# A forward scan that starts from the heads' reciprocals, in a linear attention with two expert layers behind it

## The chip, the core and the metric

The kernel runs on one core of a Trainium2 chip. The metric is the device time of one execution in microseconds (us); lower is better. Each core has TensorE (PE in the profile, PEld for its weight loads), VectorE (DVE), ScalarE (ACT), GpSimd (POOL) and SyncE (SP, which only issues transfers here). Each engine runs its own program in order and waits on semaphores.

## The reference

Three layers, cut to what matters. The output of one is the input of the next.

```python
def _attn_ref(q, k, v, alpha):                 # 4 batches, 8 heads, 768 steps, 48 wide
    for t in range(S):
        state = alpha[:, :, t, :, None] * state + np.einsum('bhd,bhe->bhde', k[:, :, t], v[:, :, t])
        y[:, :, t] = np.einsum('bhd,bhde->bhe', q[:, :, t], state)

def _moe_ref(x, w_gate, w_noise, noise, w1, w2):   # 3072 tokens of 384, 8 experts, 1024 hidden
    noisy_logits = x @ w_gate + np.log1p(np.exp(x @ w_noise)) * noise
    top2 = np.argpartition(-noisy_logits, 2, axis=1)[:, :2]     # softmax over the two gives top2_w
    ...
            h = np.maximum(x[mask] @ w1[e], 0.0)
            out[mask] += top2_w[mask, k, None] * (h @ w2[e])

def _moe2_ref(x, w_in, w_out):                 # 384 -> 2048 -> 384
    h = x @ w_in
    return np.maximum(0.01 * h, h) @ w_out
```

## The kernel before

**Scan stage.** The 3072 steps are cut into 24 units of 128 steps (4 batches of 6). A unit holds all 8 heads: 48 channels of two heads on 112 partitions, four such pairs side by side, so a tile has 4 x 128 columns. With the decays `at`, VectorE makes two products by scans: backward `suf` (tile pF), the decay from a step to the unit's end, and forward `wt` (tile pT), the decay from the unit's start. Keys are multiplied by `suf` (kt), queries by `wt` (qp). A pattern in PSUM (pC, `ends` and `begins`) restarts the scans at each head. The forward scan starts from 1, and what is needed is `wt` divided by the head's total decay; VectorE takes the reciprocals of the four totals (rec), and ScalarE scales the queries with them, one ACTIVATE for each pair (`scaled`). TensorE then makes the scores (pS), GpSimd masks them (am), and further products give the unit's output (pY), its turned form (pA) and the state's update (pM).

**Route and passage.** For each four units the two best experts of each token are chosen by a chain of some 22 small VectorE operations (names g_, lg for the logits), TensorE counts (pA), and GpSimd scatters the rows to the experts' slots in DRAM (x_s, indexes si). After the sixth such group `gidx_op` computes `gidx`, the slots for the way back, and `top2_weights` the gate's weights; `fill_ops` (`free`, freesum, ...) finds the slots that stay empty.

**Experts.** Rows of an expert are loaded, transposed by TensorE (line 641, banks pA and pB in turn), and split into a high and a low part (xh by ScalarE, xl by VectorE) for three-product matmuls: `gemm1` (ph, nine matmuls a step), `gemm2` (py, three matmuls a block). The weights come in pairs of 256 hidden columns, four pairs an expert; ScalarE makes the high part (w1h, w2h), and VectorE or GpSimd the low part by a subtraction (`split_lo`, line 501; A and B are the buffers' names). Expert 0's low parts are made by GpSimd. Two groups of each expert and a dense third layer follow, all bound to the order below.

**Order.** Nothing is scheduled by hand: each piece of work is a step with an engine, a planned duration, needs and rings of buffers, and the `Planner` lays the steps out in time, engine by engine, and emits them in that order. Durations and due times decide only the order. A step with `port=True` on VectorE or GpSimd is not laid beside another such step of the other engine. `EARLY` is 2: experts 0 and 1 have a first group that is taken before all rows are known.

Of the kernel before, what the change touches and what calls it, by code (L numbers as in the profile page):

```python
# [7 lines left out]
FT = mybir.dt.float32  # L8
# [3 lines left out]
U32 = mybir.dt.uint32  # L12
# [68 lines left out]
class Planner:  # L81

    NEAR, FAR, SLACK, RATE, LAND = 0.1, 0.25, 0.8, 0.25, 2.0
# [282 lines left out]
def tile_kernel(  # L366
# [324 lines left out]
    def build_experts(t0, R, scat, last_x, ready_at, totals, acc_done, begun):  # L691
# [36 lines left out]
        def expert_weights(i, after):  # L728
# [4 lines left out]
            for m, nm in enumerate(("w1s", "w2s")):  # L733
# [5 lines left out]
                AUX[i].append([hi, add("vg" if phase == 2 else "g", dict(v=0.87, g=1.8) if phase == 2 else 1.8, lambda en="g", m=m: split_lo(i, m, en), [hi],  # L739
# [209 lines left out]
    with ExitStack() as actx:  # L949
# [4 lines left out]
        bank = psum.tile([PP, 2, HP, C // 4], U32, name="pC", bufs=1)  # L954
        nc.vector.memset(bank, 0)
        nc.vector.memset(bank[:, 0, :, C // 4 - 1:], 1 << 24)
        nc.vector.memset(bank[:, 1, :, 0:1], 1)
        ends, begins = (bank[:, i].rearrange("p h c -> p (h c)").bitcast(mybir.dt.uint8) for i in range(2))

        def keep_busy(area, n):  # L960
# [6 lines left out]
            scr=1, rec=4, pA=1, pB=1, xg=XGB, XT=2, W=NA + NB, w1s=2, w2s=2, ph=2, hh=4, hl=4, py=4, ys=3, hc=2, f64=F64B, f64o=2).items()}  # L967
# [6 lines left out]
        def build_unit(u):  # L974
# [29 lines left out]

            def back():
                d["suf"] = psum.tile([PP, NW], FT, name="pF", bufs=1)
                nc.vector.tensor_tensor_scan(rev(d["suf"][:, :]), rev(d["at"][:, 1:NW + 1]),
                                             rev(ends), 0.0, OP.mult, OP.add)
                d["sv"] = d["suf"].rearrange("p (h c) -> p h c", c=C)

            def forth():
                d["wt"] = psum.tile([PP, NW], FT, name="pT", bufs=1)
                nc.vector.tensor_tensor_scan(d["wt"][:, :], d["at"][:, 0:NW], begins, 0.0, OP.mult, OP.add)

            def inverse():
                d["rec"] = work.tile([PP, HP], FT, name="rec", bufs=4)
                nc.vector.reciprocal(d["rec"], d["sv"][:, :, 0])

            def total():
                nc.vector.tensor_mul(tots[:, u, :], d["sv"][:, :, 0], d["at"][:, NW + 1:NW + 1 + HP])  # L1020

            b0 = b1 = add("v", 1.13, back, use=[(LA, R["at"])], takes=[R["suf"]])
# [527 lines left out]
```

## Time and profile before

| | us |
|---|---|
| median of 3 runs | 1059.86 |
| lowest and highest run | 1059.13, 1061.74 |
| profiled execution, its own time | 1063.24 |
| its span, first to last instruction | 1061.50 |
| TensorE busy in the span | 1032.2 (97%) |
| VectorE, ScalarE, GpSimd busy | 572.0, 410.0, 256.5 |

The rows come from one profiled execution; times in them run from the start of its span. The scan stage lasts until about 150 us on TensorE, the experts follow without a break. Busy time of TensorE counts pipelined matmuls from start to modelled end. Idle time of an engine that is not the bound costs nothing by itself.

### The profile page before, as it was taken

To read this page: it belongs to the slowest core of one execution; us is meant where nothing else is said; L and a number is where in the kernel's file an instruction comes from. 1 tells how busy PE (TensorE), PEld (TensorE's weight loads), DVE (VectorE), ACT (ScalarE), POOL (GpSimd) and SP (SyncE) were. 2 spreads that over 40 slices of the span, in tenths; PEclk is the share of its full clock that TensorE was granted. 3 is DMA by queue.
4 is the path that set the end of the run, shared out by engine and by line. 5 is a ranking of instruction groups with operands and counts; after the bars stand their busy time and mean duration, and the time that the engine had idled before them with its cause. 6 is when DMAs were issued, how large, how long until landed. Compare 5 with 4: busy or idle time off the path is not lost.

```text
span 1061.5 us, 18105 instructions
## 1 busy us (share of the span) xinstructions
PE 1032.2 (97%) x6808; PEld 990.7 (93%) x6808; DVE 572.0 (54%) x1170; ACT 410.0 (39%) x911; POOL 256.5 (24%) x291
## 2 busy tenths in 40 slices
PE   8999997999999999999999999999999999999997
PEld 7877787989999999999899999999999999999997
DVE  6999946324455554656464224645454545454543
ACT  6988753324344535545453222322222222222211
POOL 3266676300122231325231021402020202000000
PEclk8999998999999999999999999999999999999999
DMA  9979445533553756657476352211010101000000
GB/s 240 236 229 293 144 141 178 173 118 127 162 189 118 223 159 191 199 174 230 140 240 212 103 198 97 82 38 38 31 45 23 45 23 46 23 16 23 1 24 25
DMA packets 77988, 132.59 MB, mean 125 GB/s; under 512 B 7890, under 2 KB 55380, under 8 KB 77892
## 3 DMA queue, kind: packets, MB, share of 16 engines
q1 hardware_dynamic: 71428, 111.49, 33.7%
q0 software_dynamic: 6464, 19.86, 5.7%
q8 instruction: 55, 0.90, 0.4%
q14 instruction: 41, 0.34, 0.1%
HBM read 93.18 MB, written 38.15 MB: 124 GB/s over the span
## 4 chain that ended last, share of the span: by engine, by line
PE 84%; DMA 5%; DVE 4%; ACT 3%; issue 2%; POOL 1%; SPq 0%; ACTq 0%; POOLq 0%; DVEq 0%
PE py L826 38%; PE ph L787 37%; PE pS L1069 2%; PE pY L1136 1%; DMA w_d<-f64g 1%; PE pA L641 1%; PE pA L1158 1%; PE pY L1129 1%; DMA w1s<-in_moe_w_dram 1%; PE pB L641 1%; DMA y_d<-ys 1%; DMA w2s<-in_moe_w_dram 1%; PE pM L1104 1%; DMA at<-in_al_l_dram 1%; DVE gidx L1276 1%
## 5 line engine op out<-in xcount | busy, mean ns | idle before, releaser
L797 ACT ACTIVATE hc<-ph 128x384 f32<-128x384 f32 x128 | 62.9, 491 | 292.3 <-PE ph L787 292.3
L811 DVE SCALAR_TENSOR_TENSOR hl<-ph,hh 128x384 fp32r<-128x384 f32 (+3 forms) x128 | 76.4, 598 | 182.3 <-ACT hh L804 182.1
L800 DVE SCALAR_TENSOR_TENSOR hc<-hc 128x384 f32<-128x384 f32 x128 | 71.5, 559 | 172.4 <-ACT hc L797 172.4
L804 ACT ACTIVATE hh<-ph 128x384 fp32r<-128x384 f32 (+3 forms) x128 | 66.8, 522 | 206.5 <-PE ph L787 199.1
L826 PE MATMUL py<-w2hA,hh 128*128 128x384 f32 (+2 forms) x416 | 142.6, 343 | 0.0
L826 PE MATMUL py<-w2hB,hh 128*128 128x384 f32 (+1 forms) x416 | 141.5, 340 | 0.3 <-ACT hh L804 0.3
L826 PE MATMUL py<-w2hA,hl 128*128 128x384 f32 (+2 forms) x416 | 141.1, 339 | 0.0
L826 PE MATMUL py<-w2lA,hh 128*128 128x384 f32 (+2 forms) x416 | 141.1, 339 | 0.0
L826 PE MATMUL py<-w2hB,hl 128*128 128x384 f32 (+1 forms) x416 | 140.0, 336 | 0.0
L826 PE MATMUL py<-w2lB,hh 128*128 128x384 f32 (+1 forms) x416 | 139.7, 336 | 0.0
L787 PE MATMUL ph<-xh,w1hB 128*128 128x384 f32 (+1 forms) x384 | 133.8, 348 | 2.6 <-DVE hl L811 2.6
L787 PE MATMUL ph<-xh,w1hA 128*128 128x384 f32 (+3 forms) x384 | 135.3, 352 | 0.7 <-DVE hl L811 0.7
L787 PE MATMUL ph<-xh,w1lA 128*128 128x384 f32 (+3 forms) x384 | 133.2, 347 | 1.8 <-POOL w1lA L501 1.8
L787 PE MATMUL ph<-xh,w1lB 128*128 128x384 f32 (+1 forms) x384 | 133.3, 347 | 0.0
L787 PE MATMUL ph<-xl,w1hB 128*128 128x384 f32 (+1 forms) x384 | 133.1, 347 | 0.0
L787 PE MATMUL ph<-xl,w1hA 128*128 128x384 f32 (+3 forms) x384 | 132.9, 346 | 0.0
L849 POOL DMA_INDIRECT xg<-y_d,gidx x48 | 49.3, 1027 | 315.7 <-PE pA L641 121.5
L814 DVE TENSOR_TENSOR hl<-hc,hh 128x384 fp32r<-128x384 f32 x128 | 71.5, 559 | 12.6 <-DVE hh L806 0.9
L826 PEld LDWEIGHTS py<-w2lA,hh 128*128 128x128 f32 (+2 forms) x416 | 77.2, 186 | 1.0
L826 PEld LDWEIGHTS py<-w2hB,hh 128*128 128x128 f32 (+1 forms) x416 | 77.1, 185 | 1.1 <-ACT hh L804 0.6
L826 PEld LDWEIGHTS py<-w2hA,hh 128*128 128x128 f32 (+2 forms) x416 | 77.2, 186 | 0.8
L826 PEld LDWEIGHTS py<-w2lB,hh 128*128 128x128 f32 (+1 forms) x416 | 77.0, 185 | 0.8
(166 smaller groups left out, 1847.7 us busy)
## 6 DMA issues: line engine op xcount, KB each, us to landing
w1s<-in_moe_w_dram SPq DMA_DIRECT2D x32, 384.0 KB
w2s<-in_moe_w_dram SPq DMA_DIRECT2D x32, 384.0 KB
kq<-in_kq_l_dram SPq DMA_DIRECT2D x24, 448.0 KB
nv<-in_v_l_dram SPq DMA_DIRECT2D x24, 256.0 KB
w1s<-in_moe_w_in_dram SPq DMA_DIRECT2D x24, 256.0 KB
w2s<-in_moe_w_out_dram SPq DMA_DIRECT2D x16, 384.0 KB
at<-in_al_l_dram SPq DMA_DIRECT2D x24, 226.2 KB
xg<-x_s SPq DMA_DIRECT2D x28, 174.0 KB
```

Of the source, the lines that this page charges most:

```text
L641: pe.last = nc.tensor.transpose(p[:, d, :n], src[:n, d * 128:(d + 1) * 128], identf[:n, :n])
L787: pe.last = nc.tensor.matmul(ps[:, :n], a[:, d, fo:fo + 128], x[:, d, :n], start=i == 0, stop=i == len(seq) - 1)
L797: nc.scalar.activation(hc[:, :n], ps[:, :n], AF.Copy)
L800: nc.vector.scalar_tensor_tensor(hc[:, :n], hc[:, :n], 0.01, hc[:, :n], op0=OP.mult, op1=OP.max)
L804: nc.scalar.activation(hh[:, :n], ps[:, :n], AF.Relu)
L811: nc.vector.scalar_tensor_tensor(hl[:, :n], ps[:, :n], 0.0, hh[:, :n].bitcast(FT), op0=OP.max, op1=OP.subtract)
L814: nc.vector.tensor_sub(hl[:, :n], HT[si, "hc"][:, :n], hh[:, :n].bitcast(FT))
L826: pe.last = nc.tensor.matmul(py[:n, :], h[:, o:o + n], w[:, f % 2, :], start=(f == 0 and i == 0), stop=(f == nf - 1 and i == 2))
L849: return nc.gpsimd.indirect_dma_start(out=yg, out_offset=None, in_=y_d[0:rows, :], in_offset=bass.IndirectOffsetOnAxis(ap=gidx[:, c, kk:kk ...
L1069: pe.last = nc.tensor.matmul(d["pa", i][:, p], d["kt"][r, p], d["qp"][r, p], start=True, stop=True)
L1104: pe.last = nc.tensor.matmul(d["pu"][r, p, :], d["kN"][:, p, r], d["v"][:, 2 * p + i, 0:D], start=p == 0, stop=first, skip_group_check=True)
L1129: pe.last = nc.tensor.matmul(d["py"][64 * i:64 * i + 64, p], d["v"][:, 2 * p + i, :], d["am"][:, i, p, :], start=p == 0, stop=first, skip_ ...
```

## The change

The pattern becomes a tile `heads` of zeros whose first column of each head is written anew for each unit: first 1.0 (`ones`, a memset of 4 elements for each partition) for the backward scan, then the reciprocal of the head's total (`inverse`, which now writes into `heads`) for the forward scan. So `forth` yields the scaled `wt` at once, `scaled` is gone, and `forth` needs `inverse`, which needs `back`. `suf` is one lasting tile. Besides, the planner reckons with a landing of 5 us instead of 2 for transfers of the second phase (rows, stores, reloads), the low parts of expert 1's weights are bound to VectorE, and `gidx_op` and `top2_weights` are marked `port=True`.

```diff
-    NEAR, FAR, SLACK, RATE, LAND = 0.1, 0.25, 0.8, 0.25, 2.0
+    NEAR, FAR, SLACK, RATE, LAND = 0.1, 0.25, 0.8, 0.25, (2.0, 5.0)
...
-                st.end = max(st.end, self.dma + self.LAND)
+                st.end = max(st.end, self.dma + self.LAND[st.phase - 1])
...
-                AUX[i].append([hi, add("vg" if phase == 2 else "g", dict(v=0.87, g=1.8) if phase == 2 else 1.8, lambda en="g", m=m: split_lo(i, m, en), [hi],
+                on = "g" if e == 0 else "v" if e < EARLY else "vg"
+                AUX[i].append([hi, add(on, dict(v=0.87, g=1.8) if len(on) > 1 else dict(v=0.87, g=1.8)[on],
+                                       lambda en=on[0], m=m: split_lo(i, m, en), [hi],
...
-        bank = psum.tile([PP, 2, HP, C // 4], U32, name="pC", bufs=1)
-        nc.vector.memset(bank, 0)
-        nc.vector.memset(bank[:, 0, :, C // 4 - 1:], 1 << 24)
-        nc.vector.memset(bank[:, 1, :, 0:1], 1)
-        ends, begins = (bank[:, i].rearrange("p h c -> p (h c)").bitcast(mybir.dt.uint8) for i in range(2))
+        heads = psum.tile([PP, HP, C], FT, name="pC", bufs=1)
+        suf = psum.tile([PP, HP, C], FT, name="pF", bufs=1)
+        nc.vector.memset(heads, 0.0)
+        nc.vector.memset(suf[:, HP - 1, C - 1:], 1.0)
+        heads_f, suf_f = (t.rearrange("p h c -> p (h c)") for t in (heads, suf))
...
+            def ones():
+                nc.vector.memset(heads[:, :, 0], 1.0)
+
             def back():
-                d["suf"] = psum.tile([PP, NW], FT, name="pF", bufs=1)
-                nc.vector.tensor_tensor_scan(rev(d["suf"][:, :]), rev(d["at"][:, 1:NW + 1]),
-                                             rev(ends), 0.0, OP.mult, OP.add)
-                d["sv"] = d["suf"].rearrange("p (h c) -> p h c", c=C)
+                nc.vector.tensor_tensor_scan(rev(suf_f[:, 0:NW - 1]), rev(d["at"][:, 1:NW]), rev(heads_f[:, 1:NW]),
+                                             1.0, OP.mult, OP.add)
+
+            def inverse():
+                nc.vector.reciprocal(heads[:, :, 0], suf[:, :, 0])
 
             def forth():
-                d["wt"] = psum.tile([PP, NW], FT, name="pT", bufs=1)
-                nc.vector.tensor_tensor_scan(d["wt"][:, :], d["at"][:, 0:NW], begins, 0.0, OP.mult, OP.add)
-
-            def inverse():
-                d["rec"] = work.tile([PP, HP], FT, name="rec", bufs=4)
-                nc.vector.reciprocal(d["rec"], d["sv"][:, :, 0])
+                d["wt"] = psum.tile([PP, HP, C], FT, name="pT", bufs=1)
+                nc.vector.tensor_tensor_scan(d["wt"].rearrange("p h c -> p (h c)"), d["at"][:, 0:NW], heads_f, 0.0,
+                                             OP.mult, OP.add)
...
-            f0 = f1 = add("v", 1.13, forth, use=[(LA, R["at"])], takes=[R["wt"]])
-            iv = add("v", 0.2, inverse, [b1], use=[(b0, R["suf"])], takes=[R["rec"]])
+            f0 = add("v", 1.13, forth, [iv], use=[(LA, R["at"]), (on, R["heads"])], takes=[R["wt"]])
...
-            def scaled():
-                for p in range(HP):
-                    nc.scalar.activation(d["qp"][:, p], d["qp"][:, p], AF.Copy, scale=d["rec"][:, p:p + 1])
...
-            q0 = add("v", 0.64, queries, [f1], use=[(LK, R["kq"]), (f0, R["wt"])], takes=[R["qp"]])
-            qq = add("a", 0.72, scaled, [q0], use=[(iv, R["rec"]), (q0, R["qp"])])
+            qq = add("v", 0.6, queries, use=[(LK, R["kq"]), (f0, R["wt"])], takes=[R["qp"]])
...
-            sc = add("p", 1.09, score, use=[(kk, R["kt"]), (q0, R["qp"])], deps=[qq], takes=[R["pS"], R["pT"]], due=b + 2.4, room=room_s)
+            sc = add("p", 1.09, score, use=[(kk, R["kt"]), (qq, R["qp"])], takes=[R["pS"], R["pT"]], due=b + 2.4, room=room_s)
...
             ends = [add("v", 0.15, gidx_op, [done_of["chain", gi][-1] for gi in range(len(RGROUPS))], phase=2,
-                        due=at_unit(NCH) + 150)]
+                        due=at_unit(NCH) + 150, port=True)]
             for eng, fn in top2_weights(nc, rt, lambda: m_all, wts[:, :, 0], wts[:, :, 1], NCH, "g_"):
-                ends.append(add(eng, 0.3, fn, ends[-1:], phase=2))
+                ends.append(add(eng, 0.3, fn, ends[-1:], phase=2, port=eng == "v"))
```

What the planner makes of it is shown at three places. First, one unit on VectorE near the start, before (forward scan pT, backward scan pF, queries qp, reciprocal rec, keys kt, total decay tots):

```order
L1013 SCALAR_TENSOR_TENSOR pT<-at,pC 112x512
L1007 SCALAR_TENSOR_TENSOR pF<-at,pC 112x512
L1034 TENSOR_TENSOR qp<-kq,pT 112x512
L1017 RECIPROCAL rec<-pF 112x4
L1030 TENSOR_TENSOR kt<-kq,pF 112x512
L1020 TENSOR_TENSOR tots<-pF,at 112x4
```

and after the change:

```order
L1008 MEMSET pC 112x4
L1011 SCALAR_TENSOR_TENSOR pF<-at,pC 112x511
L1015 RECIPROCAL pC<-pF 112x4
L1034 TENSOR_TENSOR kt<-kq,pF 112x512
L1019 SCALAR_TENSOR_TENSOR pT<-at,pC 112x512
L1023 TENSOR_TENSOR tots<-pF,at 112x4
L1038 TENSOR_TENSOR qp<-kq,pT 112x512
```

The backward scan goes first, a memset stands ahead of it, and the queries come last. Second, GpSimd in the passage, from the fourth scatter (x_s) behind the first weight splits on, before:

```order
L1257 DMA x_s<-xg,si 6785x384 x4
L501 TENSOR_TENSOR w1lA<-w1s,w1hA 128x768
L1257 DMA x_s<-xg,si 6785x384
L501 TENSOR_TENSOR w2lA<-w2s,w2hA 128x768
L1257 DMA x_s<-xg,si 6785x384
L501 TENSOR_TENSOR w1lA<-w1s,w1hA 128x768
L501 TENSOR_TENSOR w2lA<-w2s,w2hA 128x768
L501 TENSOR_TENSOR w1lB<-w1s,w1hB 128x768
L501 TENSOR_TENSOR w2lA<-w2s,w2hA 128x768
L1257 DMA x_s<-xg,si 6785x384 x8
```

and after:

```order
L1256 DMA x_s<-xg,si 6785x384 x4
L501 TENSOR_TENSOR w1lA<-w1s,w1hA 128x768
L1256 DMA x_s<-xg,si 6785x384
L501 TENSOR_TENSOR w2lA<-w2s,w2hA 128x768
L1256 DMA x_s<-xg,si 6785x384
L501 TENSOR_TENSOR w1lA<-w1s,w1hA 128x768
L501 TENSOR_TENSOR w2lA<-w2s,w2hA 128x768
L1256 DMA x_s<-xg,si 6785x384
L501 TENSOR_TENSOR w2lA<-w2s,w2hA 128x768
L1256 DMA x_s<-xg,si 6785x384 x7
```

The second w1lA of this piece is that of pair 3. The run behind it has lost w1lB, the first split of expert 1, and a scatter stands in its place. Third, TensorE at the count matmul (from acc and ones_b) whose result `free` reads, before:

```order
L578 MATMUL pA<-acc,ones_b 128x8
L826 MATMUL py<-w2hA,hh 112x384
L826 MATMUL py<-w2lA,hh 112x384
L826 MATMUL py<-w2hA,hl 112x384
L826 MATMUL py<-w2hA,hh 112x384
L826 MATMUL py<-w2lA,hh 112x384
L826 MATMUL py<-w2hA,hl 112x384
L641 MATMUL pA<-identf,xg 128x128 x3
```

After the change 18 such py rows and nine ph rows stand behind the count; the last of the nine and the transpositions are:

```order
L789 MATMUL ph<-xh,w1hA 128x336
L789 MATMUL ph<-xl,w1hA 128x336
L789 MATMUL ph<-xh,w1lA 128x336
L641 MATMUL pA<-identf,xg 128x128 x3
L641 MATMUL pB<-identf,xg 128x128 x3
```

The transposition into pA, which needs the bank that `free` reads, has moved 21 matmuls away from the count. On VectorE `gidx` and `free` still stand directly behind the last slots (si) and a subtraction for the expert.

## Rows read from the trace of the kernel before

**Rows 1.** Stretches: from:to, length, busy by engine (instructions), TensorE clock, DMA share, GB/s.

```profile
0.00:138.00 138.00, 128.38 (x1637) 109.32 (x1638) 119.89 (x282) 108.19 (x293) 69.94 (x116) 0.96 0.78 224
138.00:180.00 42.00, 34.27 (x265) 31.95 (x265) 20.84 (x56) 14.69 (x32) 30.46 (x25) 0.92 0.47 156
180.00:1054.00 874.00, 868.12 (x4903) 848.38 (x4902) 431.28 (x833) 285.63 (x585) 156.14 (x151) 1.00 0.34 108
```

**Rows 2.** Waits of TensorE up to 200 us: total, times, longest.

```profile
PE pA L641 <- DVE free L582: 4.9, 1, 4.9
PE ph L787 <- POOL w1lA L501: 1.8, 1, 1.8
```

**Rows 3.** Chain that ended last, behind 170 us: start, length, what.

```profile
171.26 2.88 PE py L826 x9
...
174.14 2.29 PE ph L787 x9
176.43 1.59 PE py L826 x9
```

**Rows 4.** Stretches of TensorE alone: length, busy, granted clock, DMA share, GB/s.

```profile
12.40:19.00 6.60, 6.60 (x56) 0.50 1.03 253
...
175.00:176.00 1.00, 1.00 (x5) 0.50 0.50 115
```

**Rows 5.** VectorE in order of time: start, length, line, operation, tiles.

```profile
164.05 6.08 DVE L1276 SCALAR_TENSOR_TENSOR gidx<-pk_all,cm_all 128x48 uint32<-128x48 f32 x1
...
170.15 0.15 DVE L582 TENSOR_SCALAR free<-pA 128x8 f32<-128x8 f32 x1
```

**Rows 6.** GpSimd in order of time, the same stretch.

```profile
163.71 0.99 POOL L1257 DMA_INDIRECT x_s<-xg,si  x1 [0.17 <-issue]
...
168.25 1.81 POOL L501 TENSOR_TENSOR w1lB<-w1s,w1hB 128x768 fp32r<-128x768 f32 x1
```

**Rows 7.** Groups up to 160 us: busy, mean ns | idle before, releasers.

```profile
L1038 ACT ACTIVATE qp<-qp,rec 112x128 f32<-112x128 f32 x96 | 30.6, 394 | 7.9 <-DVE rec L1017 6.6 <-DVE qp L1034 0.9 <-DVE g_z L264 0.3
```

**Rows 8.** Groups of VectorE up to 138 us, as above.

```profile
L1017 DVE RECIPROCAL rec<-pF 112x4 f32<-112x4 f32 x24 | 4.1, 172 | 0.1
...
L284 DVE TENSOR_REDUCE cm_all<-g_ca 128x4 f32<-128x32 f32 x10 | 1.9, 186 | 0.3
...
L956 DVE MEMSET pC<- 112x4 uint32 x1 | 0.1, 62 | 0.1
```

**Rows 9.** VectorE in order of time, an early unit and the last.

```profile
22.48 1.20 DVE L1007 TENSOR_TENSOR_SCAN pF<-at,pC 112x512 f32<-112x512 f32 x1
23.78 0.18 DVE L1017 RECIPROCAL rec<-pF 112x4 f32<-112x4 f32 x1
23.88 0.13 DVE L1020 TENSOR_TENSOR tots<-pF,at 112x4 f32<-112x4 f32 x1
...
134.39 0.68 DVE L1030 TENSOR_TENSOR kt<-kq,pF 112x512 f32<-112x512 f32 x1
```

**Rows 10.** Waits of VectorE up to 138 us.

```profile
DVE lg L1167 <- ACT xg L1162: 5.4, 8, 1.7
DVE pT L1013 <- DMA at<-in_al_l_dram: 5.1, 2, 2.9
...
DVE lg L1167 <- PE pA L1158: 1.1, 2, 0.6
```

**Rows 11.** TensorE in order of time, the end of the scan stage.

```profile
138.00 1.16 PE L1069 MATMUL pS<-qp,kt 48*128 48x128 f32 x16
...
140.17 1.09 PE L1129 MATMUL pY<-am,nv 128*64 128x128 f32 x16
...
149.52 0.40 PE L787 MATMUL ph<-xh,w1hA 128*128 128x336 f32 x1
...
153.78 0.34 PE L826 MATMUL py<-w2hA,hh 128*112 128x384 f32 x1
```

**Rows 12.** TensorE in order of time, the rows of expert 2.

```profile
212.19 0.52 PE L641 MATMUL pA<-identf,xg 116*128 116x116 f32 x3 [0.72 <-DVE xl L650]
```

More of the change, by code (lines that the diff above doesn't have):

```diff
@@ L966, in tile_kernel @@
             at=5, kq=4, nv=5, suf=1, wt=1, kt=4, qp=4, pM=1, kN=2, pS=1, pT=1, ar=2, am=2, sp=2, S=2, pY=1, xt=XTB,
-            scr=1, rec=4, pA=1, pB=1, xg=XGB, XT=2, W=NA + NB, w1s=2, w2s=2, ph=2, hh=4, hl=4, py=4, ys=3, hc=2, f64=F64B, f64o=2).items()}
+            scr=1, heads=1, pA=1, pB=1, xg=XGB, XT=2, W=NA + NB, w1s=2, w2s=2, ph=2, hh=4, hl=4, py=4, ys=3, hc=2, f64=F64B, f64o=2).items()}
         add = plan.add
@@ L1022, in build_unit @@
-            b0 = b1 = add("v", 1.13, back, use=[(LA, R["at"])], takes=[R["suf"]])
-            tt = add("v", 0.12, total, [b1], use=[(LA, R["at"]), (b0, R["suf"])])
+                d["wt"] = psum.tile([PP, HP, C], FT, name="pT", bufs=1)
+                nc.vector.tensor_tensor_scan(d["wt"].rearrange("p h c -> p (h c)"), d["at"][:, 0:NW], heads_f, 0.0,
+                                             OP.mult, OP.add)
+            def total():
+                nc.vector.tensor_mul(tots[:, u, :], suf[:, :, 0], d["at"][:, NW + 1:NW + 1 + HP])
@@ L1024, in build_unit @@
+            on = add("v", 0.07, ones, takes=[R["heads"]])
+            b0 = add("v", 1.13, back, use=[(LA, R["at"]), (on, R["heads"])], takes=[R["suf"]])
+            iv = add("v", 0.1, inverse, use=[(b0, R["suf"]), (on, R["heads"])])
+            tt = add("v", 0.09, total, use=[(LA, R["at"]), (b0, R["suf"])])
             totals.append(tt)
-            f0 = f1 = add("v", 1.13, forth, use=[(LA, R["at"])], takes=[R["wt"]])
-            iv = add("v", 0.2, inverse, [b1], use=[(b0, R["suf"])], takes=[R["rec"]])
+            f0 = add("v", 1.13, forth, [iv], use=[(LA, R["at"]), (on, R["heads"])], takes=[R["wt"]])
@@ L1040, in build_unit @@
-            kk = add("v", 0.64, keys, [b1], use=[(LK, R["kq"]), (b0, R["suf"])], takes=[R["kt"]])
-            q0 = add("v", 0.64, queries, [f1], use=[(LK, R["kq"]), (f0, R["wt"])], takes=[R["qp"]])
-            qq = add("a", 0.72, scaled, [q0], use=[(iv, R["rec"]), (q0, R["qp"])])
+                nc.vector.tensor_mul(d["qp"], d["kq"][:, 1], d["wt"])
+            kk = add("v", 0.59, keys, use=[(LK, R["kq"]), (b0, R["suf"])], takes=[R["kt"]])
+            qq = add("v", 0.6, queries, use=[(LK, R["kq"]), (f0, R["wt"])], takes=[R["qp"]])
@@ L1095, in decay @@
                     nc.gpsimd.tensor_mul(d["sp"], prev["S"], tots[:, u, :, None].to_broadcast([PP, HP, D]))
-                dc = add("g", 0.42, decay, [tt], use=[(prev["step"], R["S"])], takes=[R["sp"]], port=True)
+                dc = add("g", 0.47, decay, [tt], use=[(prev["step"], R["S"])], takes=[R["sp"]], port=True)
             if not last:
@@ L1142, in build_unit @@
             if not first:
-                done = add("p", 1.01, across, [w0, qq], use=[(q0, R["qp"]), (dc, R["sp"]), (w0, R["pY"])],
+                done = add("p", 1.01, across, [w0], use=[(qq, R["qp"]), (dc, R["sp"]), (w0, R["pY"])],
                            due=b + PERIOD + 5)
```

4 lines of the change are left out of this document (1 added, 3 removed).

## The prediction

> **What bounds the kernel now.** I read the stretches first, to see where TensorE is not busy. From 180 us to the last product it misses 5.9 of 874; before 138 it misses 9.6 us, and between 138 and 180 it misses 7.7 with a mean granted clock of 0.92 [rows 1]. So the experts' part is TensorE's own work, and what lies behind 1054 us is the last store, and the change can only win in the first 180 us, the scan stage and the passage from it to the experts. In the scan stage VectorE is nearly as full as TensorE: 119.89 of 138 us [rows 1].
>
> Next the waits of TensorE up to 200 us. The longest is one of 4.9 us: a transposition of expert rows into the bank pA waited for VectorE's `free`. The second, 1.8 us, waited for a weight split (w1lA) on GpSimd [rows 2]. Before the long wait TensorE ran at its full clock of 2.4 GHz; behind it the granted clock was 0.50 of that, 1.2 GHz, up to 176 us, and nine products that take 1.59 us at the full clock took 2.88 us [rows 3, 4].
>
> Then I looked at what `free` waited for. It stands on VectorE behind `gidx`, a tiny operation that lasted from 164.05 to 170.13 [rows 5]. In those 6.08 us GpSimd ran a scatter and then three weight splits with nothing between them, of 1.8 us each; the last ended at 170.06 [rows 6]. `gidx` came through exactly when GpSimd's run of splits was over, so the 4.9 us are a collision of VectorE and GpSimd, and the halved clock is its consequence.
>
> **The passage, the sure part.** Three edits meet here. `gidx` and the operations on the gate's weights are marked as users of the shared port, so the planner lays no GpSimd step beside them; expert 1's splits may run on VectorE alone, which takes the split w1lB out of GpSimd's run (VectorE, busy 20.84 of 42 us there [rows 1], has room for it); and the new order moves TensorE's steps. The listings show the result: `gidx` still stands behind the last slots of the route, but GpSimd's run behind the scatter is two splits and then a scatter, and TensorE has 18 products (py) and 9 (ph) between the count and the transposition that needs `free`, where it had 6 py.
> If `gidx` meets the run again at the same point, it ends with the second split, 1.8 us after the end of the split of pair 3 (w1lA). TensorE's last 9 ph ahead of the transposition need that same split, and they take some 1.4 us (27 of them stood between 149.52 and 153.78 together with nothing else, 0.158 us each [rows 11]). So what is left of the 4.92 us is about 0.4, wherever the run lies; if `gidx` is free of the run, nothing. I take 4.5 us.
> The clock gives back more. The products at 171.26 lost 2.88 less 1.59, 1.3 us; those at 174.14 took 2.29 where nine at 0.158 take 1.42, 0.9 us; the transposition ahead some 0.3 [rows 3]. That is 2.5 us, and **the passage gives 7.0 us**, at most 7.4.
> The Trainium skill says in "SBUF — State Buffer", section "Who interferes with whom", that an instruction with two SBUF inputs on VectorE and a GpSimd instruction that reads SBUF exclude each other, the second blocking until the first is done. By that rule `gidx` would have waited for one split, 1.8 us at most, while the trace shows three. By the rule nothing would be left of the wait now, and the passage would give 7.4 instead of 7.0.
> The 1.8 us behind w1lA [rows 2] I leave as they are: GpSimd's order is unchanged up to that split (two splits, one, four scatters, this one), and the whole row hangs on the same slots of the route as TensorE's way there.
>
> **The scan stage, the unsure part.** Removed are 24 times four ScalarE operations, 30.6 us of ScalarE [rows 7]. They lie between the forward scan and the scores, but ScalarE is not the bound: it is busy 108.19 of 138 us [rows 1]. Added to VectorE is one memset of 4 elements for each unit; the scans, the reciprocal and the two products stay. What is new is the order of need: memset, backward scan, reciprocal, forward scan, queries, each needing the one before. Before, the two scans had no need of each other.
> The trace has this price. Behind a backward scan of 1.20 us that ended at 23.68, the reciprocal that needs it began at 23.78, 0.10 after its end; the next operation, which does not need the reciprocal, began 0.07 before the reciprocal's end [rows 9]. A need costs 0.17 us. For each unit: a memset, 0.06 [rows 8], with the backward scan 0.10 behind it, together 0.16; the reciprocal right behind its scan, 0.17; the queries behind the forward scan, 0.17 less the 0.08 of a small product that mostly stands between, 0.09. The sum is 0.42, and 24 units make 10.1 us. From below it is the memsets alone, 24 by 0.06 or 1.5 us; from above, three full needs and the memset for each unit, 24 by 0.57 or 13.7 us.
> The Trainium skill says in "VectorE: DVE Perf Modes", section "The DRAIN you can't avoid", that a semaphore between chained operations costs nothing extra, since the pipe is emptied anyhow. The rows just read differ. By the rule only the 1.5 us of memsets are added, and that case is a rival below.
> What takes this up is VectorE's own idle time. It waited 5.4 us for ScalarE's copies ahead of the logits (lg), 1.1 us in the same place for TensorE, and 5.1 us for the first loads of decays, of which some 2.2 lie ahead of the first scan [rows 10]. A slower VectorE meets the loads and copies later, and ScalarE, 30.6 us lighter, copies sooner: 9.4 us could be recovered, I take 8. So VectorE comes 2.1 us later to its end.
> The last unit counts. Before, its keys were ready at 135.07 [rows 9], behind 14 small operations of the fifth route and one subtraction for the expert; in the new listing its last operand, the queries, has 9 of them and no subtraction ahead. Five at 0.22 (0.19 and the gap [rows 8]) and 0.5 make 1.6 us. So the operand is ready at 135.07 + 2.1 - 1.6 = 135.6, and the last score can start at 135.7 instead of 138.00 [rows 11], 2.3 earlier. Of that about 0.9 is lost again: the route's count matmul is four steps further on TensorE, and VectorE has 11 small operations and two subtractions of 0.5 to do for it behind the queries, 3.6 us, while TensorE needs 1.16 + 0.6 + 1.1 to get there. **The scan stage ends 1.4 us earlier**; in general its end moves by the added time less the recovered less 3.5.
>
> **Edits that I cost at nothing.** The later landing (5 us instead of 2 for transfers of the second phase) changes TensorE's order behind the passage at three places: one pair of steps swapped, the transpositions ahead of the dense layer later by a step or two, and those of expert 2 closer together. The first two are hidden by TensorE's queue, which has 5.9 us of gaps in 874 [rows 1]. For the third there is a price: the transpositions into two banks already waited 0.72 us for VectorE's subtraction [rows 12], and one product of 0.5 us fewer stands between them. I add 0.5 us. The load of values is one place earlier on SP, which could shorten the first gap; taken as nothing.
>
> **Sum.** 7.0 + 1.4 - 0.5 = 7.9 us. The profiled execution took 1063.24 us for a span of 1061.50, the median of the runs is 1059.86; so 1055.3 in such an execution and **1052.0 us** in the median. A change under 0.3%, 3.2 us, can't be told from none.
>
> **The rivals.**
> *VectorE becomes the bound of the scan stage.* Its logits' waits stay, because the copies wait for TensorE and not for ScalarE, and only 4 us are recovered. The stage ends 10.1 - 4 - 3.5 = 2.6 us later; 7.0 - 2.6 - 0.5 = 3.9 us, 1056.0. For it speaks that VectorE is 87% busy [rows 1]; against it that most of those waits name ScalarE. Chance 0.20.
> *The collision is only moved.* `gidx` is not let in at the scatter between the second and the third split: it ends 1.8 + 1.0 + 1.8 = 4.6 us after the split that TensorE's 9 ph need, TensorE waits 3.2 us, and the clock falls again. The passage gives 1.7 us, in all 2.6, 1057.3. For it speaks that `gidx` was already held during the scatter ahead of the splits [rows 5, 6]. Chance 0.10.
> *Slower.* The small operations on VectorE's new chain are held up as others are: the memset and reciprocal write into PSUM while scans read it, and each unit pays 1.0 us instead of 0.42. Then 24 - 8 - 3.5 = 12.5 us are lost in the scan stage, and 1065.9 comes out; it turns slower than 3.2 us from 0.88 us a unit on. Against it: 24 reciprocals have a mean of 172 ns, with no long one to pull it up [rows 8]. Chance 0.07.
> *Needs cost nothing.* Only the memsets are added. 1.5 - 8 - 3.5 would be 10 us earlier, but TensorE can't follow: it has 9.6 us of idle time in 138 [rows 1], a part of it ahead of its first work. I take 4 us of it: 7.0 + 4 - 0.5 = 10.5, 1049.4. The reciprocal at 23.78 speaks against it [rows 9]. Chance 0.06. The section on the DRAIN in the Trainium skill's page "VectorE: DVE Perf Modes" would have it so.
> *The early clock stays up.* Behind the gaps of the start, TensorE worked without a pause from 12.4 to 19.0 us at a granted clock of 0.50, 1.2 GHz [rows 4]; half of the 6.6 us is lost. If the earlier start of unit 1 avoids that, 3.3 us come on top: 1048.7. Chance 0.07.
>
> **How the numbers follow.** My forecast has a chance of 0.50 and its own range of 1048.5 to 1056, from 6 to 9.4 us recovered and 8 to 12 added. The range of 1046.5 to 1058.5 takes in all but the slow rival and the outer parts of the second and last. Faster than 1056.7: nearly all of the forecast, the two fast rivals, half of the first and a little of the second, 0.75. Slower than 1063.0: the slow rival, 0.06. The rest, 0.19, is no change.
>
> **What the profile after will show.** The passage: `gidx` at 4 us or less, no wait of TensorE for `free` above 0.5 us, and the clock at 1.00 from 160 to 180. The scan stage: reciprocals some 0.10 behind the end of the backward scan; VectorE busier than 87% of the stage, with less waiting at lg; ScalarE near 78 us busy; the first ph between 146 and 149.5. From 220 us on the two traces should run in step. I am wrong if the first ph comes later than 150, or if `free` is still what a transposition waits for.

## The result and the profile after

The changed kernel takes 1048.53 us in the median, against 1060.8 for the kernel before beside it: a ratio of 0.9886, interval 0.9861 to 0.9912. A second set gave 0.9909 (0.9883 to 0.9934). So it is some 10 to 12 us faster; forecast were 7.9, with 1052.0 us and a range of 1046.5 to 1058.5. The profiled execution took 1047.05 us (span 1045.3), 16.2 less than the one of before (1063.24), which lay high among its kind (four timed runs of it gave 1059.13 to 1062.08).

Stretches of the changed kernel, columns as in [rows 1], the last up to its last product:

```profile
0.00:138.00 138.00, 126.83 (x1678) 107.22 (x1678) 125.43 (x307) 85.76 (x200) 72.27 (x119) 0.99 0.83 227
138.00:180.00 42.00, 39.54 (x280) 37.05 (x276) 26.96 (x64) 19.46 (x38) 33.36 (x29) 1.00 0.63 207
180.00:1038.00 858.00, 855.59 (x4847) 837.33 (x4846) 421.01 (x821) 278.37 (x573) 157.90 (x149) 1.00 0.33 107
```

From 0 to 138 us ScalarE has lost 22 us of work, VectorE is busy for 125.4 us instead of 119.9, and the granted clock is 0.99 instead of 0.96. From 138 to 180 TensorE is busy for 39.5 instead of 34.3 us at a full clock. Behind 180 us it misses 2.4 of 858 us; before it was 5.9 of 874. Waits of TensorE up to 200 us:

```profile
PE pA L1230 <- DVE lg L1166: 3.9, 3, 1.5
...
PE ph L789 <- DVE acc L1219: 1.2, 1, 1.2
```

The two rows of [rows 2] are gone, `free` and w1lA. Where the one for w1lA was, 1.2 us ahead of a ph are left; the waits ahead of the route's rank product (L1230) for `lg`, all in the scan stage, have grown from 1.5 us to 3.9. The passage on VectorE, then on GpSimd, then on TensorE:

```profile
159.85 4.38 DVE L1275 SCALAR_TENSOR_TENSOR gidx<-pk_all,cm_all 128x48 uint32<-128x48 f32 x1
164.16 0.15 DVE L582 TENSOR_SCALAR free<-pA 128x8 f32<-128x8 f32 x1
```

```profile
160.50 1.86 POOL L501 TENSOR_TENSOR w1lA<-w1s,w1hA 128x768 fp32r<-128x768 f32 x1
162.30 1.85 POOL L501 TENSOR_TENSOR w2lA<-w2s,w2hA 128x768 fp32r<-128x768 f32 x1
164.32 0.99 POOL L1256 DMA_INDIRECT x_s<-xg,si  x1 [0.17 <-issue]
```

```profile
160.30 0.17 PE L578 MATMUL pA<-acc,ones_b 128*128 128x8 bf16 x1
...
164.94 0.49 PE L641 MATMUL pA<-identf,xg 128*128 128x128 f32 x3
```

`gidx` still meets the run, but the run ends with its second split at 164.15, and `gidx` at 164.23; the scatter behind it begins at 164.32. `free` is done at 164.31, and the transposition into pA, 27 matmuls behind the count, begins at 164.94 without a wait. This is the passage as forecast (rows 5, 6 and 3 of before answer to it).

To see where the time came from I read one and the same matmul in both traces: the first ph, the 163rd and the last.

| profiled execution | first ph | first to 163rd | 163rd to last |
|---|---|---|---|
| before | 149.52 | 67.40 | 833.36 |
| changed | 146.61 | 60.81 | 826.66 |
| difference | 2.9 | 6.6 | 6.7 |
| forecast | 1.4 | 6.5 | 0 |

The 0.5 us that I took off for expert 2 belongs to the middle stretch, since its transpositions come before the 163rd ph (212.19 and 216.92 us before).

The last stretch is a surprise. Waits of TensorE behind 200 us, before and then changed:

```profile
PE ph L787 <- DVE hl L811: 3.3, 3, 1.8
PE pB L641 <- DVE xl L650: 1.3, 1, 1.3
PE pA L641 <- DVE xl L650: 0.7, 1, 0.7
```

```profile
PE pA L641 <- DVE xl L650: 1.6, 2, 0.9
PE pA L641 <- PE pB L641: 0.8, 1, 0.8
```

Before, these and two of 0.3 us made 5.9. The 0.7 and one of the 0.3 belong to expert 2's transpositions, ahead of the 163rd ph, as do 1.6 of the changed kernel's 2.4. So 4.8 us stand against 0.9 behind it. Besides, before had a granted clock of 0.50 from 531.0 to 534.4 us, which cost some 1.7 us; the changed kernel has no such place there. About 1 us of the 6.7 is left that I can't place.

The largest step, 3.5 us, lies near 530 us. VectorE, then TensorE, before:

```profile
529.55 0.56 DVE L834 COPY ys<-py 116x384 f32<-116x384 f32 x1 [3.48 <-issue]
530.02 0.55 DVE L811 SCALAR_TENSOR_TENSOR hl<-ph,hh 128x384 fp32r<-128x384 f32 x1
```

```profile
530.62 0.44 PE L787 MATMUL ph<-xh,w1hB 128*128 128x384 f32 x1 [1.76 <-DVE hl L811]
```

The subtraction `hl` stood on VectorE behind a copy of results (ys), ahead of which VectorE was idle for 3.48 us, and its operand `hh` was ready at 528.34 at the latest. The halved clock follows that wait. The place of the 1.3 us shows the same of `xl`, before:

```profile
293.60 0.96 DVE L501 TENSOR_TENSOR w2lB<-w2s,w2hB 128x768 fp32r<-128x768 f32 x1 [2.34 <-ACT w2hB L497]
294.47 0.51 DVE L650 TENSOR_TENSOR xl<-pB,xh 128x348 fp32r<-128x348 f32 x1
```

```profile
295.04 0.52 PE L641 MATMUL pB<-identf,xg 116*128 116x116 f32 x3 [1.30 <-DVE xl L650]
```

and changed:

```profile
281.31 0.52 DVE L650 TENSOR_TENSOR xl<-pB,xh 128x348 fp32r<-128x348 f32 x1
284.43 0.96 DVE L501 TENSOR_TENSOR w2lB<-w2s,w2hB 128x768 fp32r<-128x768 f32 x1 [2.60 <-ACT w2hB L497]
```

```profile
284.10 0.46 PE L641 MATMUL pB<-identf,xg 116*128 116x116 f32 x3
```

Before, the subtraction `xl` stood on VectorE behind one for w2lB, whose weights had just landed; now `xl` comes first, at 281.31, and TensorE's transposition at 284.10 waits for nothing. This order is the planner's, and the edit that moves it is the landing of 5 us, whose moves behind the passage I had costed at nothing.

### The profile page after: what moved, and what is told of

It reads as the page before. It is cut to its first block, busy times and chain, and to the rows that moved or that the text cites. A ratio compares the mean times of both kernels' runs of the same rounds, so it can differ in the third digit from the quotient of the medians.

```text
span 1045.3 us, 18038 instructions
## 1 busy us (share of the span) xinstructions
PE 1023.1 (98%) x6800; PEld 982.5 (94%) x6800; DVE 573.4 (55%) x1190; ACT 385.1 (37%) x814; POOL 263.5 (25%) x295
## 4 chain that ended last, share of the span: by engine, by line
PE 87%; DMA 5%; DVE 5%; ACT 1%; issue 1%; SPq 0%; DVEq 0%; ACTq 0%
PE py L828 40%; PE ph L789 39%; DMA at<-in_al_l_dram 2%; PE pY L1128 1%; DMA kq<-in_kq_l_dram 1%; PE pA L641 1%; PE pA L1157 1%; PE pY L1135 1%; PE pB L641 1%; PE pS L1068 1%; DMA w2s<-in_moe_w_dram 1%; DMA nv<-in_v_l_dram 1%; DVE pF L1011 0%; PE pM L1107 0%; PE pM L1103 0%
## 5 line engine op out<-in xcount | busy, mean ns | idle before, releaser
L799 ACT ACTIVATE hc<-ph 128x384 f32<-128x384 f32 x128 | 62.9, 491 | 289.6 <-PE ph L789 287.0
```

The lines of the kernel that those rows point to most:

```text
L799: nc.scalar.activation(hc[:, :n], ps[:, :n], AF.Copy)
```

## The experiments

Three sets, each with its own runs of the kernel before beside it (medians 1061.5, 1060.15 and 1056.48 us, on three chips). A gain over the kernel before is worked out from the ratio; two kernels of one set are compared by their medians. My theory after the result: the landing gives all behind 220 us, in the passage the landing (a later transposition) and the split binding (a shorter run) each take part of one wait, and the scan's restart itself may be worth nothing. Rivals: the late waits were chance; the restart gives the 2.9 us.

**Landing alone.**

```diff
-    NEAR, FAR, SLACK, RATE, LAND = 0.1, 0.25, 0.8, 0.25, 2.0
+    NEAR, FAR, SLACK, RATE, LAND = 0.1, 0.25, 0.8, 0.25, (2.0, 5.0)
...
-                st.end = max(st.end, self.dma + self.LAND)
+                st.end = max(st.end, self.dma + self.LAND[st.phase - 1])
```

> The kernel before with one edit, the landing of 5 us in the planner's second phase. Theory (order): the transposition into pA that needs `free` now stands 15 py and 9 ph behind the count instead of 6 py, 3.0 us further, and GpSimd's run still holds three splits, so its wait falls from 4.9 us to about 2; behind 220 us VectorE and ScalarE take the rows of an expert ahead of weights that have not landed, and the later waits for xl and hl (0.7 to 1.8 us each) and the halved clock near 531 us are gone, 6 us. In all 8 to 11.5 us faster than before, 1049 to 1053. Rival (chance of the loads): the later waits belong to one execution and not to the order; then only the passage gains, 3 to 5.5 us, and waits for xl or hl of 4 us in all stand in the profile behind 220 us. Rival (nothing): the planner's numbers move no wait; within 1 us of before.

Measured: 1051.33 us, 0.9902 (0.988 to 0.9923), 10.4 us faster. One constant gives most of the whole change. VectorE and GpSimd in its passage:

```profile
161.13 6.17 DVE L1247 SCALAR_TENSOR_TENSOR si<-pk_all,cm_all 128x8 uint32<-128x8 f32 x1 [0.18 <-issue]
...
167.64 0.19 DVE L1276 SCALAR_TENSOR_TENSOR gidx<-pk_all,cm_all 128x48 uint32<-128x48 f32 x1
```

```profile
165.46 1.81 POOL L501 TENSOR_TENSOR w1lB<-w1s,w1hB 128x768 fp32r<-128x768 f32 x1
```

Here it was `si`, ahead of `gidx`, that met the run; it ended at 167.30, when the third split did (167.27). The wait for `free` was 2.2 us, as expected, and no wait above 0.3 us was left behind 220 us.

**Split binding and marks alone.**

```diff
+                on = "g" if e == 0 else "v" if e < EARLY else "vg"
...
-                        due=at_unit(NCH) + 150)]
+                        due=at_unit(NCH) + 150, port=True)]
```

> The kernel before with the two passage edits alone: expert 1's low parts on VectorE, and the port marks. The transposition stays 6 py behind the count. Theory: `gidx` ends with the second split of GpSimd's run instead of the third, 1.8 us earlier; the wait for `free` falls from 4.9 to about 3.1 us and the clock falls to 0.50 behind it all the same; 1.5 to 2.5 us faster. Rival (my prediction's credit for these two edits and the order together): `gidx` is let in at once by the marks, the wait is under 0.5 us, 7 us faster. Rival (only moved): `gidx` is held over the scatter and one more split, the wait stays at 4.9 us or grows, no change.

Measured: 1056.68 us, 0.9946 (0.9926 to 0.9965), 5.7 us faster, more than the theory's 1.5 to 2.5 and less than the rival's 7.

```profile
164.94 3.94 DVE L1278 SCALAR_TENSOR_TENSOR gidx<-pk_all,cm_all 128x48 uint32<-128x48 f32 x1
```

```profile
167.00 1.81 POOL L501 TENSOR_TENSOR w2lA<-w2s,w2hA 128x768 fp32r<-128x768 f32 x1
```

```profile
PE pA L641 <- DVE free L582: 1.5, 1, 1.5
```

`gidx` took 3.94 us and ended at 168.88 with the second split (168.81), as the theory has it; but the wait was 1.5 us, not 3.1, and the clock, at 0.50 from 162 to 165 us, was 0.99 in the ten behind that. Besides, 18 products and not 6 stood between expert 2's transpositions, and their 1.0 us of waits was gone. The rule of the run holds; what the wait costs also hangs on where TensorE is when the run begins, which I had not priced.

**Restart alone**, with the two other edits taken back.

```diff
+            def ones():
+                nc.vector.memset(heads[:, :, 0], 1.0)
...
-            qq = add("a", 0.72, scaled, [q0], use=[(iv, R["rec"]), (q0, R["qp"])])
+            qq = add("v", 0.6, queries, use=[(LK, R["kq"]), (f0, R["wt"])], takes=[R["qp"]])
```

> The kernel before with the restart from the reciprocals alone (memset, new order of need, no scaling on ScalarE). Theory: the scan stage behaves as in the changed kernel, the first ph comes 2.9 us earlier than in the kernel before, with the granted clock at 1.00 from 12 to 19 us; the wait for `free` stays, 4.9 less about 0.5 us for three more py ahead, and the clock falls to 0.50 behind it; the waits behind 220 us stay. 2.5 to 4 us faster. Rival (the early clock is chance): the clock falls at 12 us here too, and the stage ends as before or up to 0.5 us later; within 1 us of before. Rival (the restart carries the gain): 7 us or more faster.

Measured: 1058.65 us, 0.9978 (0.9961 to 0.9994), 2.3 us faster: small, but more than nothing. The first ph came at 148.30, and the clock fell at 16.7 us all the same, so neither the theory nor its first rival fits; the wait for `free` was 3.9 us, where 4.4 were expected. Its middle stretch is 66.21 us, 1.2 shorter than before.

**The changed kernel without the landing.**

```diff
-    NEAR, FAR, SLACK, RATE, LAND = 0.1, 0.25, 0.8, 0.25, (2.0, 5.0)
+    NEAR, FAR, SLACK, RATE, LAND = 0.1, 0.25, 0.8, 0.25, 2.0
```

> The changed kernel with the landing of 2 us everywhere. Theory (three separate gains): the first ph 2.9 us earlier; the transposition stands 9 py behind the count, `gidx` ends with the second split, so about 2.5 us of wait and the halved clock stay; the waits behind 220 us stay. 5 to 6.5 us faster than before, so 6 us slower than the changed kernel. Rival (landing does nothing): as the changed kernel, 12 us faster. Rival (the split and the marks give all of the passage): 9.5 to 10.5 us faster.

Measured: 1055.99 us, 0.9936 (0.9913 to 0.9958), 6.8 us faster than before (5.5 by the medians). Its late stretch is 831.06 us, 4.4 longer than the changed kernel's. Its first ph, at 150.88, is the latest of the first six traces though its scans are the new ones, with the clock at 0.50 from 15.8 to 22.6 us: the restart does not keep the early clock up.

**The changed kernel without the restart** (the old scans and `scaled`, all else changed; no diff beyond the one shown).

> The kernel before with the landing, the split binding and the port marks, but the old scans and ScalarE's scaling: the changed kernel without its headline. Theory (the restart is worth nothing in the end of the scan stage; the 2.9 us in the profiled pair were an early halved clock that falls or doesn't fall by execution): landing alone gave 10.4 us and left 2.2 us of wait for `free`, which the shorter run of splits takes away, so 12 to 13 us faster than before, level with the changed kernel within 1 us. Rival (my prediction's term, 1.4 us from the stage): 1 to 2 us slower than the changed kernel. Rival (2.9 us from the stage, as the pair of traces has it): 3 us slower than the changed kernel or more.

Measured: 1050.13 us, 0.9899 (0.9878 to 0.992), beside 0.9909 for the changed kernel in the same set; the theory had 12 to 13 us over the kernel before, and it is 10.7. Level: without the restart the kernel is 0.2 us faster by the medians, inside the intervals, and beside the other edits no gain of the restart shows. VectorE does wait less with it. Its longest waits up to 138 us in this kernel, and then in the changed kernel's second trace:

```profile
DVE lg L1169 <- ACT xg L1164: 7.0, 8, 3.8
DVE pT L1015 <- DMA at<-in_al_l_dram: 3.6, 2, 2.4
```

```profile
DVE lg L1166 <- ACT xg L1161: 3.3, 4, 1.8
DVE pF L1011 <- DMA at<-in_al_l_dram: 2.4, 1, 2.4
```

**The changed kernel without the split binding.**

```diff
-                on = "g" if e == 0 else "v" if e < EARLY else "vg"
...
+                AUX[i].append([hi, add("vg" if phase == 2 else "g", dict(v=0.87, g=1.8) if phase == 2 else 1.8, lambda en="g", m=m: split_lo(i, m, en), [hi],
```

> The changed kernel with expert 1's low parts on either engine as before, so the run of GpSimd behind the scatter is three splits again; the transposition stays 18 py and 9 ph behind the count. Theory (the lock is held for the whole run): `gidx` or the `si` ahead of it ends with the third split, 1.8 us later than in the changed kernel, where the transposition began 0.6 us behind `free`; so a wait of about 1.2 us, and 1 to 3 us slower than the changed kernel, by whether the clock falls. Rival (one split blocks): no wait, level with the changed kernel. Rival (the split binding carries the passage): 5 us slower or more.

Measured: 1052.77 us, 0.9925 (0.9901 to 0.9949), 2.4 us slower than the changed kernel beside it. That is the size that the theory of the run has, but the two intervals overlap, so the time alone does not show it. The trace does, VectorE, GpSimd and TensorE:

```profile
162.41 7.93 DVE L1273 SCALAR_TENSOR_TENSOR gidx<-pk_all,cm_all 128x48 uint32<-128x48 f32 x1
```

```profile
168.47 1.79 POOL L501 TENSOR_TENSOR w2lA<-w2s,w2hA 128x768 fp32r<-128x768 f32 x1
```

```profile
170.47 0.55 PE L641 MATMUL pA<-identf,xg 128*128 128x128 f32 x3 [2.81 <-DVE free L582]
```

With the run now four splits, `gidx` lasted 7.93 us and ended at 170.34; the fourth split ended at 170.26.

**Six memsets a unit.**

```diff
-                nc.vector.memset(heads[:, :, 0], 1.0)
+                for _ in range(6):
+                    nc.vector.memset(heads[:, :, 0], 1.0)
```

> The changed kernel with six memsets of the heads' columns a unit instead of one, in the same order on every engine. Each more costs VectorE between 0.06 us (its duration) and 0.16 us (with a gap behind it), so 24 x 5 x 0.06 to 0.16 = 7 to 19 us in all. Theory (VectorE bounds the scan stage, with some 5 us of its idle time still to be had up to 138 us): 2 to 14 us slower than the changed kernel, and the first ph later by as much. Rival (TensorE bounds it, VectorE has room): within 1 us of the changed kernel.

Measured: 1068.91 us, 1.0084 (1.0061 to 1.0107), 18.5 us slower than the changed kernel beside it, above the theory's 14.

```profile
51.27 0.61 DVE L1009 MEMSET pC<- 112x4 f32 x5
51.93 0.15 DVE L1024 TENSOR_TENSOR tots<-pF,at 112x4 f32<-112x4 f32 x1
```

Five memsets and the gap behind them take 0.66 us, 0.13 each, so 120 more are 15.8 us; the first ph came 16.5 later (164.75 against 148.24). So what VectorE gets more to do in the changed kernel's scan stage costs as much as it takes. On TensorE the 16.5 us are 8.0 of more idle time up to the last score (18.7 us against 10.6) and 8.5 lost to more time at a clock of 0.50 (23.9 us of it against 6.8), so half of the price is the clock's.

**The changed kernel again.**

> The changed kernel once more, beside the three above, for their differences. Theory: 1048 to 1050 us, with the clock at 12 to 19 us by chance. Rival: it differs from its first runs by more than 2 us.

Measured: 1050.36 us, 0.4 above the range expected and 1.8 from its first runs; first ph at 148.24, then 61.32 and 827.05 us.

**Landing for the passage only, and for what is behind it only**, both on the kernel before.

```diff
-                st.end = max(st.end, self.dma + self.LAND)
+                st.end = max(st.end, self.dma + (5.0 if st.phase == 2 and t0 < 190 else self.LAND))
```

> The kernel before with the landing of 5 us only for second-phase transfers that the planner lays before 190 us of its own time: the transposition moves to 15 py and 9 ph behind the count, GpSimd's order is as before, behind the passage nearly all is as before. Theory: the passage gives what it gave in the trace of landing alone, 5 us (2.7 of the wait for `free`, the rest from a clock that needn't fall), and the waits behind 220 us stay; 4 to 6 us faster than before. Rival (the passage gives little without the shorter run of splits): under 3 us.

```diff
+                st.end = max(st.end, self.dma + (self.LAND if t0 < 190 else 5.0))
```

> The kernel before with the landing of 5 us only for second-phase transfers that the planner lays from 190 us of its own time on: the passage is as before (transposition 6 py behind the count), VectorE's and ScalarE's order behind it is changed. Theory: the waits for xl and hl behind 220 us (5.9 us in the trace of before) fall under 2.5 us, 4 to 6 us faster than before; the wait for `free` of some 4.9 us stays. Rival (those waits were chance): within 1 us of before.

Measured: 1053.72 us, 0.9973 (0.9959 to 0.9987), and 1053.6 us, 0.9967 (0.9951 to 0.9982): 2.8 and 2.9 us by the medians, in a set in which the kernel before was faster than in the others. Both are under the 4 to 6 expected, and together they are 5.7 us, where landing alone gave 10.4 in its own set; landing alone was not timed beside them, so whether the two add up is open. Waits of TensorE from 155 us on, first passage only, then late only:

```profile
PE ph L787 <- DVE hl L811: 3.7, 3, 1.9
...
PE pB L641 <- DVE xl L650: 1.2, 1, 1.2
PE pA L641 <- DVE free L582: 0.9, 1, 0.9
```

```profile
PE pA L641 <- DVE free L582: 4.9, 1, 4.9
PE ph L787 <- DVE hl L811: 1.6, 1, 1.6
```

The traces part the two cleanly. Passage only has a wait for `free` of 0.9 us and all the late ones, a passage of 62.92 and a late stretch of 833.61; late only has the whole 4.9 us for `free`, a passage of 67.38 and a late stretch of 828.72, with 3.6 us of waits left behind 200 us. Behind 220 us they are 2.6, and the waits for `xl` and `hl`, of which I had expected under 2.5, are 1.6. Why the timed gains are smaller than these stretches say, I could not settle: no trace of the kernel before was taken in that set.

**Without the port marks.**

```diff
-                        due=at_unit(NCH) + 150, port=True)]
+                        due=at_unit(NCH) + 150)]
```

> The changed kernel without the port marks on `gidx` and the gate's weights: no row of TensorE and GpSimd moves, twelve rows of VectorE do. Theory (the marks change no order that counts): level with the changed kernel within 1 us. Rival (the weights' operations beside GpSimd's splits hold `freesum` up): 2 us slower than the changed kernel or more.

Measured: 1049.34 us, 0.992 (0.9896 to 0.9945); the changed kernel itself was not in this set, and its other sets gave 0.9886 and 0.9909. No effect shows.

**A landing of 8 us.**

```diff
-    NEAR, FAR, SLACK, RATE, LAND = 0.1, 0.25, 0.8, 0.25, (2.0, 5.0)
+    NEAR, FAR, SLACK, RATE, LAND = 0.1, 0.25, 0.8, 0.25, (2.0, 8.0)
```

> The changed kernel with a landing of 8 us in the second phase instead of 5: the transposition into pA moves further behind, and weights are laid later still on VectorE and ScalarE. Theory (the remaining waits for xl are of the same kind): 0 to 2 us faster than the changed kernel. Rival (too late: rows or weights now come late for TensorE): 2 us slower or more.

Measured: 1073.59 us, 1.0161 (1.0132 to 1.019), the rival's way. TensorE in the dense layer:

```profile
695.00 0.66 PE L789 MATMUL ph<-xh,w1hA 128*128 128x384 f32 x1 [7.56 <-DMA w1hA<-w_d]
```

At 620 us its ph still stand within 1 us of the changed kernel's; then TensorE waits 8.2 us for `hh` and `hl` on VectorE between 665 and 683 us and 8.8 for the dense layer's prepared weights (w_d), with a mean clock of 0.60 in the 13 us from 687 on. The landing is a number with a good value between two worse ones, not a direction. No version was clearly faster than the changed kernel; landing alone, without the restart and without the marks are level with it inside the intervals.

## Why the prediction was right, and where not

**The passage: right, in place and size.** Forecast 6.5 us (7.0 less 0.5 for expert 2), and 6.6, 6.1 and 5.1 in three traces (first ph to 163rd: 67.40 before, then 60.81, 61.32 and, without the marks, 62.28). Each sub-step held: `gidx` is not let in at once, it ends with the second split, and the moved transposition covers the rest. The 0.5 us came as priced: with three products fewer between expert 2's transpositions, the waits there are 1.56 us instead of 1.03. One term was left out: the 1.8 us for w1lA, which I left as they were, are 1.2 us in every trace with the new scans and 1.8 in every one with the old. What I had not parted is which edit does what. In the same stretch the traces have 66.2 to 67.4 with neither landing nor split binding, 62.9 with the landing alone, 65.0 with landing and restart, where the run had grown to four splits, 61.8 and 62.0 with the split binding and no landing, 60.8 to 63.0 with both. Either edit by itself takes most of the gain, so their gains don't add up. The marks, which I counted among the three edits, do nothing that shows.

On the rule that the Trainium skill gives in "SBUF — State Buffer", section "Who interferes with whom", that the second of two such instructions blocks until the first is done: the runs decide against reading it as one instruction. `gidx` or `si` was held over two, three and four splits in a row and came through within 0.1 us of the end of the last (3.94, 6.17 and 7.93 us). In the record each split of a run begins 0.04 to 0.08 us before the one ahead of it has ended, so no gap stands between them.

**The scan stage: the terms were too large, and cancelled.** I had 10.1 us added on VectorE and 8 recovered. From the start of the first scan to the end of the last operand, with gaps over 0.25 us counted as waits, VectorE was occupied for 120.9 us on average in the six traces with the old scans and for 124.9 in the seven with the new (six memsets left out). The six small operations that no longer stand ahead of the last operand (1.6 us by my own price) make it 5.6 us added, 0.23 a unit instead of 0.42. Its waits fell from 8.9 to 4.2 us on average, 4.7 recovered instead of 8. An early unit, where nothing else stands on VectorE, before and then changed:

```profile
3.75 1.23 DVE L1013 TENSOR_TENSOR_SCAN pT<-at,pC 112x512 f32<-112x512 f32 x1 [2.25 <-DMA at<-in_al_l_dram]
...
7.33 1.22 DVE L1013 TENSOR_TENSOR_SCAN pT<-at,pC 112x512 f32<-112x512 f32 x1
```

```profile
7.76 0.06 DVE L1008 MEMSET pC<- 112x4 f32 x1
7.85 1.23 DVE L1011 TENSOR_TENSOR_SCAN pF<-at,pC 112x511 f32<-112x511 f32 x1
9.12 0.19 DVE L1015 RECIPROCAL pC<-pF 112x4 f32<-112x4 f32 x1
9.21 0.67 DVE L1034 TENSOR_TENSOR kt<-kq,pF 112x512 f32<-112x512 f32 x1
9.81 1.22 DVE L1019 TENSOR_TENSOR_SCAN pT<-at,pC 112x512 f32<-112x512 f32 x1
...
11.05 0.69 DVE L1038 TENSOR_TENSOR qp<-kq,pT 112x512 f32<-112x512 f32 x1
11.75 0.06 DVE L1008 MEMSET pC<- 112x4 f32 x1
```

From start to start it is 3.58 us before and 3.99 now: 0.41 more, so here my price is right. In later units operations of the route stand between, as seven do between the memset at 59.95 us and its scan at 61.58, and there the need costs nothing. That this makes the mean 0.23 is my reading; no run tests it. The reciprocal begins 0.03 us behind the end of the backward scan, not 0.10, in all 18 units in which it follows directly. By the Trainium skill's "VectorE: DVE Perf Modes", section "The DRAIN you can't avoid", the semaphore of a need costs nothing beside the drain that there is anyhow. Here a need costs some 0.12 us, 0.03 behind the end instead of 0.09 ahead of it, between the rule and my 0.17.

The net was to be 1.4 us; of the 0.9 in it for the last route's count, my own terms give only 0.7. The step that failed lies at the last unit: I let the last score start 0.1 us behind its last operand. VectorE and TensorE of the changed kernel:

```profile
130.81 0.68 DVE L1038 TENSOR_TENSOR qp<-kq,pT 112x512 f32<-112x512 f32 x1
```

```profile
134.81 0.38 PE L1068 MATMUL pS<-qp,kt 48*128 48x128 f32 x2
```

The stretch between them, columns as in [rows 4]:

```profile
131.49:134.81 3.32, 3.32 (x52) 1.00 0.18 64
```

TensorE has 3.3 us of earlier work in hand there and does not pause, and it waits for nothing longer than 0.15 us from 112.3 us on. In the seven traces the score starts 3.3 to 3.8 us behind the operand, in the six with the old scans 2.4 to 2.9. So the operand comes 0.6 us earlier on average (132.9, not 133.5) and the score 0.2 us later: the net does not show, and the timing with and without the restart is level.

The first ph comes at 147.5 us on average in those six traces and at 148.1 in the seven. The 2.9 us of the profiled pair are mostly the clock: up to the first ph it stood at 0.50 for 10.2 us in the trace of before, for 3.4 in the changed one, and for 0 to 13.7 in all of them. With half of that time taken off, the first ph lies between 142.1 and 144.9 in each of the thirteen, at 143.8 on average with the old scans and 144.0 with the new. Late landing only, with the old scans, has no such time, and its first ph came at 143.03, the earliest. The rival "the early clock stays up" thus came true in the changed kernel's first trace, but not by the change: its second trace has the fall, at 16.7 us, and landing alone, with the old scans, has none there.

**Edits costed at nothing: the step that failed.** I wrote that the change can only win in the first 180 us, and that two of the landing's moves behind the passage "are hidden by TensorE's queue, which has 5.9 us of gaps in 874". The late stretch is 826.0 to 827.1 us in the seven traces with the landing everywhere and 830.6 to 833.6 in the five without it behind the passage; landing late only lies between, at 828.7. That is 3.5 to 7.6 us won in the traces, of which 1.7 in the two longest is a clock at 0.50 near 525 us, behind a wait for `hl`. My reading of the order was of TensorE's alone. The 5.9 us were not a cover but, nearly all of them, waits for `xl` and `hl`, and the order that the edit moves is VectorE's and ScalarE's. By the timing, landing late only gave 2.9 us.

So the sum came out near by two errors of opposite sign: the scan stage's 1.4 us did not show, and the landing's moves behind the passage, put at nothing, gave 3 us by the timing and more in the traces, and made the change larger than the 7.9 forecast. That 1048.53 still lies in the range is partly luck: it is the fast edge of my own 1048.5 to 1056, which I had reached by waits recovered in the scan stage and not by a gain behind the passage. The rival "VectorE becomes the bound" is half borne out: more work on VectorE is paid, as the six memsets show, and 4.7 us were recovered, nearer to its 4 than to my 8; but the added time was 5.6 us and not 10.1, and at the stage's end it is TensorE that has work in hand. Whether VectorE was the bound before, no run tests. Nothing was seen of the slow rival, the reciprocals' mean being 191 ns. Of the signs that I named, `free` no longer waited for, the clock at 1.00 from 160 to 180, less waiting at lg and the first ph at 146.61 came as said; `gidx` at 4.38 us instead of 4 or less, and ScalarE at 85.8 us instead of 78, did not, and from 220 us on the traces did not run in step.

## What to carry to other kernels

Where a table of planned times sets the order, look at the order of every engine behind the place you study, and ask of each wait that is left in the "full" part for whom it waits: the 5.9 us of gaps in 874 here held a gain as large as the passage's. A tiny VectorE operation between two SBUF tiles costs whatever run of GpSimd operations it happens to meet, so shorten the run or move away who needs the result; doing both gives little more than one. Price a change by a run without it as well: the edit that gave this change its name was worth 2.3 us alone and, beside the other edits, nothing that could be measured.

## What the runs showed of the hardware

An operation of VectorE with two SBUF inputs that met GpSimd's splits was let in only when a run of them had ended: 3.94 us over two, 6.17 over three, 7.93 over four, and `freesum` 2.13 us at a single one. The 0.01 to 0.03 us between a scatter's end and the first split did not let it in. Two operations with one SBUF input were held by a single split as well, `g_ws` for 1.51 us (173.47, passage alone) and a copy of the gate's weights for 1.50 (169.50, landing alone). A subtraction `hl`, with an input from PSUM, took its usual 0.51 us beside a split (159.52, landing alone). The granted clock of the first 120 us differs between executions of the same kernel: the changed one had a fall to 0.50 at 16.7 us in one trace and none there in the other, with the first ph 1.6 us apart.
